# Weight splits moved from GpSimd to VectorE in half tiles, and the weight conversion spread into the second layer

## The chip, the cores and the metric

The kernel runs on one core of one Trainium2 chip. The time is the device time of one execution in microseconds, the lower the better. A core has TensorE (PE), VectorE (DVE), ScalarE (ACT), GpSimd (POOL) and SyncE (SP, which here only issues transfers). Each works through its own instructions in order, and semaphores join them.

## The reference

Three steps follow each other, all with float32 data:

```python
# attention: 4 batches, 8 heads, 576 tokens, head size 64; each query sees the 64 keys up to its own
attn = softmax(where(mask, q @ k.T / 8, -1e9)) @ v          # -> x: 2304 tokens x 512
# experts: a token goes to one of 8; 288 places each, given out in the order of the logits
logits = x @ w_gate                                          # 2304 x 8
assigned = greedy(sorted(logits))
out[assigned == e] = maximum(x[assigned == e] @ w1[e], 0) @ w2[e]      # 512 -> 1024 -> 512
# gated layer
g, val = x @ moe2_w_gate, x @ moe2_w_val                     # 512 -> 1536
return (g * sigmoid(g) * val) @ moe2_w_out                   # 1536 -> 512
```

The three `moe2` weights come as float64 bits and are turned into float32 on the chip.

## The kernel before

The order of all instructions on each engine is the order in which the Python code writes them. There are four stages.

**Attention** (up to about 125 us) makes x, transposed, in `big`, and the logits. The change doesn't touch it.

**Routing** (`routing`, some 125 to 164 us) finds each token's place in six rounds (`step`). A round is a chain of small VectorE steps: `M`, `m`, `below`, `Us`, `u`, `G`; then 18 small TensorE products into `cnt`, then `sat` on VectorE, then two more small products, whose results give VectorE `lt` and ScalarE `cg`, from which GpSimd makes the next `U` (`narrow`). `beside(it)` stands behind each round and holds work that fills gaps: rows of x are transposed and stored to DRAM (`store_rows`), and weights are split. `assign` follows the last round (`oh`, then `ranks`, `places`, `indices`), then a gather of rows by GpSimd, and a branch that is normally not taken.

**Experts** (`experts`, 173 to 401 us): for each of 8 experts `e` and 8 blocks `f` of 128 hidden units, `first(e, f)` makes 12 products of 288 columns into `psw`; ScalarE and VectorE make from it the two parts `hh` and `hl` (`split_psum`). `second` of the `f` before makes 12 products into the four `psa`. At even `f` a piece of the next expert's rows is transposed on TensorE and becomes `xt`.

**Gated layer** (`gated`, 401 to 848 us): three groups `g` of 768 tokens, 12 `f`, two blocks `b` of 384 tokens each. `block` makes 12 products into a `psg` (pg), ScalarE's sigmoid and a VectorE step `sg` read it, then 12 products into the other `psg` (pv), which a second VectorE step reads; ScalarE and VectorE make the two parts of `p`. There are two `psg` banks, so each has to be read before the second product behind it starts. `second` of the `f` before adds 18 products of 512 columns into six `pso`.

Two kinds of work on the weights run beside these stages.

*The split* (`Stream`): every weight matrix is used as two float32r parts, `whi` (a rounded copy by ScalarE) and `wlo` (what is left, a subtraction). A tile of 128x1024 is loaded into one of four `wraw` buffers and split in two halves of 128x512; `whi` and `wlo` have nine buffers each. For the experts' weights the second half's subtraction runs on GpSimd, the first on VectorE; for the gated layer's both run on VectorE. `need(key)` splits up to five tiles ahead of the one asked for. In routing, `beside` splits one tile per round from the second round on, both halves on GpSimd. There are 64 tiles of the experts' weights and 18 of the gated layer's, which are loaded and split anew for each group.

*The conversion* (`convert`, `convert_move`): 36 half pieces of the gated layer's weights; each is loaded as bits (`raw64`), takes four VectorE steps on 128x512 (lines 936 to 942) and a square on ScalarE, and is stored to DRAM, from where the stream loads it. Six steps stand right behind the branch, two or three after each `f` in experts 0 to 6, and `convert_rest` does what is left ahead of expert 7 and closes its buffers.

Of the kernel before, what the change touches and what calls it, by code (L numbers as in the profile page):

```python
# [21 lines left out]
class Stream:  # L22
    """Weights: loaded in float32, split on chip into two float32r parts whose sum is exact."""

    def __init__(self, ctx, tc):
        self.nc = tc.nc
        self.raw = ctx.enter_context(tc.tile_pool(name="wraw", bufs=4))
        self.todo, self.raws, self.parts = [], [], {}
        self.nload = self.nsplit = 0

    def open(self, ctx, tc):
        self.hi = ctx.enter_context(tc.tile_pool(name="whi", bufs=9))
        self.lo = ctx.enter_context(tc.tile_pool(name="wlo", bufs=9))
# [4 lines left out]
    def load(self, upto):  # L38
        while self.nload < min(upto, len(self.todo)):
# [6 lines left out]
    def split(self, upto, engine=None):  # L46
        upto = min(upto, len(self.todo))
        self.load(upto + 4)
        while self.nsplit < upto:
            key, _ = self.todo[self.nsplit]  # L50
            t = self.raws[self.nsplit]
            h = self.hi.tile(list(t.shape), F32R, name="whi")
            lo = self.lo.tile(list(t.shape), F32R, name="wlo")
            for s in range(2):
                if len(t.shape) == 3 and t.shape[1] % 2 == 0:
                    m = t.shape[1] // 2
                    sl = (slice(None), slice(s * m, s * m + m))
# [3 lines left out]
            self.parts[key] = (h, lo)  # L61
            self.nsplit += 1


class Kernel:
# [29 lines left out]

    def attention(self, ctx):
# [16 lines left out]
        # additive masks over [query, (block before, own block)], and without a block before  # L113
# [10 lines left out]
        for i in (1, 5):  # L124
            n = 3
# [16 lines left out]
        # A unit is a window of 64 queries of one pair of heads, hp and hp + HP. A group is four units.  # L142
# [6 lines left out]
        def load_qk(b, name, j):  # L149
            """On the partitions of a quadrant 32 tokens, and 32 of d."""  # L150
# [1037 lines left out]
```

## Time and profile before

| | us |
|---|---|
| runs shown (3) | median 856.53, 856.20 to 856.91 |
| span of the profiled execution, first to last instruction | 854.2 |
| TensorE busy | 796.9 (93%) |
| VectorE busy | 542.7 (64%) |
| ScalarE busy | 383.4 (45%) |
| GpSimd busy | 225.3 (26%) |

The span is the time base of every start in the rows below; the time of a run is some 2.3 us longer than it. A row of a timeline has the start, the length, the engine, the line of the kernel, the operation, the tile written and the tiles read, and the count of instructions that are merged in it; in brackets stands how long the engine was idle just before, and what ended that. TensorE's matmuls overlap, so their lengths add up to more than the distance of their starts.

### The profile page before, as it was taken

How to read it: one execution, taken by the hardware profiler on the slowest of the kernel's cores; microseconds unless marked ns; L12 is line 12 of the kernel's file. 1: busy time of each engine (PE TensorE's matmuls, PEld its weight loads, DVE VectorE, ACT ScalarE, POOL GpSimd, SP SyncE). 2: the span in 40 equal slices, each digit the busy share in tenths (PEclk: the TensorE clock that was granted, in tenths of full speed). 3: DMA queues.
4: the chain of work that ended last, by engine and by line, in shares of the span. 5: the costliest groups of instructions: out<-in, count | busy, mean ns of one | idle time of the engine just before them, and what ended most of it. 6: DMA issues, size and time to landing. Idle time of an engine off the chain costs nothing.

```text
span 854.2 us, 14581 instructions
## 1 busy us (share of the span) xinstructions
PE 796.9 (93%) x5411; PEld 738.6 (86%) x5411; DVE 542.7 (64%) x1014; ACT 383.4 (45%) x980; POOL 225.3 (26%) x263
## 2 busy tenths in 40 slices
PE   5879895499999999999999999999999999999996
PEld 4668774299999999999999999999999999999996
DVE  5868888789999999976443444554344454433422
ACT  4777875356555665666322323433222343221311
POOL 6765745544455444440000000020000002000002
PEclk9999997599999999999999999999999999999998
DMA  9999935679999998855311222241122224101001
GB/s 141 137 142 144 195 113 177 186 243 312 290 318 307 302 315 287 285 187 174 99 29 46 74 74 74 75 149 35 41 74 74 75 74 148 43 32 50 1 1 74
DMA packets 137931, 119.50 MB, mean 140 GB/s; under 512 B 88896, under 2 KB 105280, under 8 KB 137856
## 3 DMA queue, kind: packets, MB, share of 16 engines
q1 hardware_dynamic: 134976, 109.09, 47.2%
q0 software_dynamic: 2880, 9.44, 3.6%
q8 instruction: 44, 0.72, 0.4%
q14 instruction: 31, 0.25, 0.1%
HBM read 99.63 MB, written 18.87 MB: 139 GB/s over the span
## 4 chain that ended last, share of the span: by engine, by line
issue 36%; PE 24%; DVE 16%; POOL 2%; ACT 1%; DMA 0%; POOLq 0%; DVEq 0%; ACTq 0%
PE psg L983 13%; DVE wlo L60 6%; PE pso L983 5%; PE psa L983 3%; PE psw L983 3%; DVE t L940 2%; DVE hl L973 2%; DVE t L938 2%; POOL out_dram L1123 2%; DVE t L936 2%; DVE t L942 1%; DVE xt L976 1%; ACT whi L58 0%; PE psw L1015 0%; DMA w<-t 0%
## 5 line engine op out<-in xcount | busy, mean ns | idle before, releaser
L983 PE MATMUL psg<-y,whi 128*128 128x384 f32 x1152 | 223.1, 336 | 0.0
L983 PEld LDWEIGHTS psg<-y,whi 128*128 128x128 f32 x1152 | 201.6, 188 | 0.0
L1123 POOL DMA_INDIRECT out_dram<-orow,idx x18 | 17.3, 963 | 443.5 <-ACT orow L1121 271.6
L983 PE MATMUL pso<-whi,p 128*128 128x512 f32 x432 | 133.3, 390 | 0.0
L60 DVE TENSOR_TENSOR wlo<-wraw,whi 128x512 fp32r<-128x512 f32 x167 | 129.6, 820 | 4.5 <-ACT whi L58 4.1
L58 ACT ACTIVATE whi<-wraw 128x512 fp32r<-128x512 f32 x236 | 130.4, 620 | 0.1
L60 POOL TENSOR_TENSOR wlo<-wraw,whi 128x512 fp32r<-128x512 f32 x69 | 100.0, 1459 | 103.4 <-ACT whi L58 40.2
L1100 DVE TENSOR_TENSOR sg<-sg,psg 128x384 f32<-128x384 f32 x72 | 39.9, 554 | 131.7 <-ACT sg L1099 131.7
L983 PE MATMUL psg<-y,wlo 128*128 128x384 f32 x576 | 123.4, 336 | 0.0
L1105 ACT ACTIVATE p<-sg 128x384 fp32r<-128x384 f32 x72 | 37.8, 525 | 152.7 <-DVE sg L1103 150.5
L983 PEld LDWEIGHTS psg<-y,wlo 128*128 128x128 f32 x576 | 102.5, 188 | 2.8 <-DVE sg L1100 0.2
L1099 ACT ACTIVATE sg<-psg 128x384 f32<-128x384 f32 x72 | 35.4, 491 | 147.0 <-PE psg L983 147.0
L983 PEld LDWEIGHTS pso<-whi,p 128*128 128x128 f32 x432 | 80.6, 188 | 14.5
L983 PE MATMUL pso<-wlo,p 128*128 128x512 f32 x216 | 84.2, 390 | 0.0
L983 PE MATMUL psa<-hl,whi 128*128 128x288 f32 x256 | 78.4, 306 | 5.2 <-DVE hl L973 4.8
L1103 DVE TENSOR_TENSOR sg<-sg,psg 128x384 f32<-128x384 f32 x72 | 39.9, 554 | 66.5 <-PE psg L983 66.2
L983 PE MATMUL psw<-xt,whi 128*128 128x288 f32 x512 | 78.4, 295 | 0.0
L983 PE MATMUL psa<-hh,whi 128*128 128x288 f32 x256 | 75.4, 295 | 0.0
L983 PE MATMUL psa<-hh,wlo 128*128 128x288 f32 x256 | 75.4, 295 | 0.0
L983 PEld LDWEIGHTS psw<-xt,whi 128*128 128x128 f32 x512 | 71.3, 188 | 0.0
L1106 DVE TENSOR_TENSOR p<-sg,p 128x384 fp32r<-128x384 f32 x72 | 40.2, 559 | 42.6 <-ACT p L1105 42.0
L245 ACT ACTIVATE pp<-ps_s,nm 128x128 f32<-128x128 f32 x144 | 51.0, 369 | 26.8 <-DVE nm L238 24.6
(179 smaller groups left out, 1157.9 us busy)
## 6 DMA issues: line engine op xcount, KB each, us to landing
wraw<-in_moe_w_dram SPq DMA_DIRECT2D x64, 512.0 KB
wraw<-w SPq DMA_DIRECT2D x54, 512.0 KB
w<-t SPq DMA_DIRECT2D x36, 256.0 KB
raw<-in_moe_w_gate_dram SPq DMA_DIRECT2D x12, 512.0 KB
raw<-in_moe_w_val_dram SPq DMA_DIRECT2D x12, 512.0 KB
raw<-in_moe_w_out_dram SPq DMA_DIRECT2D x12, 512.0 KB
vw<-in_v_dram SPq DMA_DIRECT2D x32, 144.0 KB
xrows<-row SPq DMA_DIRECT2D x18, 256.0 KB
```

The source lines that it names most:

```text
L58: self.nc.scalar.activation(h[sl], t[sl], AF.Copy)
L60: eng.tensor_tensor(lo[sl], t[sl], h[sl].bitcast(F32), op=OP.subtract)
L245: nc.scalar.activation(PP[g][:, u, :], ps[:, u, :], AF.Exp, bias=nm[:, u:u + 1], scale=scale, accum_out=SM[g][:, u:u + 1])
L936: nc.vector.tensor_scalar(t, hi, 0x07FFFFFF, 3, op0=OP.bitwise_and, op1=OP.logical_shift_left)
L938: nc.vector.scalar_tensor_tensor(t, hi, -0x40000000, t, op0=OP.bitwise_and, op1=OP.bitwise_or)
L983: self.nc.tensor.matmul(acc, x, y, start=start and i == 0, stop=stop and i == len(seq) - 1)
L1099: nc.scalar.activation(sg, pg, AF.Sigmoid)
L1100: nc.vector.tensor_tensor(sg, sg, pg, op=OP.mult)
L1103: nc.vector.tensor_tensor(sg, sg, pv, op=OP.mult)
L1105: nc.scalar.activation(p[0][:, sl], sg, AF.Copy)
L1106: nc.vector.tensor_tensor(p[1][:, sl], sg, p[0][:, sl].bitcast(F32), op=OP.subtract)
L1123: d = nc.gpsimd.indirect_dma_start(out=self.out, out_offset=bass.IndirectOffsetOnAxis(ap=self.idx[:, 6 * g + t:6 * g + t + 1], axis=0), in ...
```

## The change

- `Stream.split` is taken apart: `half` splits the next half tile, always with ScalarE and VectorE; GpSimd takes no part. `split` calls `half` until enough is done.
- In routing, each of the six rounds has one `half`, written between the products into `cnt` and `sat`. `beside` splits nothing any more, and behind the branch `split(6)` stands where six conversion steps stood.
- `need` runs four tiles ahead in place of five, and `whi` and `wlo` have seven buffers in place of nine. The conversion's buffers stay to the end of the kernel; the rows' buffers (`xg`) are closed ahead of expert 7.
- The conversion has one step after each `f` of all eight experts, and two where `f` is 3 or 7. The rest, four steps each, follows the blocks of the gated layer until it is done. `limit` keeps the stream from loading a piece that is not stored yet.
- The comments and doc lines are gone, which shifts line numbers by some lines.

```diff
     def open(self, ctx, tc):
-        self.hi = ctx.enter_context(tc.tile_pool(name="whi", bufs=9))
-        self.lo = ctx.enter_context(tc.tile_pool(name="wlo", bufs=9))
+        self.hi = ctx.enter_context(tc.tile_pool(name="whi", bufs=7))
+        self.lo = ctx.enter_context(tc.tile_pool(name="wlo", bufs=7))
...
-    def split(self, upto, engine=None):
-        upto = min(upto, len(self.todo))
-        self.load(upto + 4)
-        while self.nsplit < upto:
...
-                self.nc.scalar.activation(h[sl], t[sl], AF.Copy)
-                eng = engine or (self.nc.gpsimd if s and key[0] in ("w1", "w2") else self.nc.vector)
-                eng.tensor_tensor(lo[sl], t[sl], h[sl].bitcast(F32), op=OP.subtract)
+    def half(self):
+        if self.nsplit == len(self.todo):
+            return
+        self.load(self.nsplit + 5)
+        key, _ = self.todo[self.nsplit]
+        t = self.raws[self.nsplit]
+        if key not in self.parts:
+            self.parts[key] = [p.tile(list(t.shape), F32R, name=n) for p, n in ((self.hi, "whi"), (self.lo, "wlo"))]
+        h, lo = self.parts[key]
+        m = t.shape[1] // 2
+        sl = (slice(None), slice(self.nhalf * m, self.nhalf * m + m))
+        self.nc.scalar.activation(h[sl], t[sl], AF.Copy)
+        self.nc.vector.tensor_tensor(lo[sl], t[sl], h[sl].bitcast(F32), op=OP.subtract)
+        self.nhalf = 1 - self.nhalf
+        self.nsplit += not self.nhalf
+
+    def split(self, upto):
+        while self.nsplit < min(upto, len(self.todo)):
+            self.half()
...
             def beside(i):
-                self.st.split(i, self.nc.gpsimd)
                 self.store_rows(3)
                 self.convert_move()
...
                 mm(cnt, G[:, c, :], bl[:, c, :], start=c == 0, stop=c == NT - 1)
+            if it < first:
+                self.st.half()
             nc.vector.tensor_scalar(self.sat[0:32], cnt[:, 0:NE], cnt[:, NE:NE + 1], 0.5 - CAP,
...
+        if self.halves:
+            st.limit = lambda: 8 * NE + self.stored // 2 if self.stored < len(self.halves) else len(st.todo)
...
-        self.st.split(self.order[key] + 5)
+        self.st.split(self.order[key] + 4)
...
         self.convert_move()
-        self.convert(6)
+        self.st.split(6)
...
             if e == NE - 1:
-                self.convert_rest()
+                self.xg_ctx.close()
...
-                if e < NE - 1:
-                    self.convert(n)
-                elif f in (1, 4):
+                self.convert(2 if f % 4 == 3 else 1)
+                if e == NE - 1 and f in (1, 4):
                     self.ready(f // 4)
...
+                self.convert_move()
                 block(g, f, p, 0)
+                self.convert()
                 if f == 11 and g < 2:
                     self.ready(2 * g + 3)
+                self.convert_move()
                 block(g, f, p, 1)
+                self.convert()
```

GpSimd in routing, before: the steps that make the `U` of the third and the fourth round, and the two halves of the first tile between them (`wraw_1485` is the tile, `cg` what the round found).

```order
L673 TENSOR_TENSOR U_2124<-U_2047,cg_2116 128x88
L673 TENSOR_TENSOR U_2124<-U_2047,cg_2116 128x56
L673 TENSOR_TENSOR U_2124<-U_2124,cg_2116 128x88
L673 TENSOR_TENSOR U_2124<-U_2124,cg_2116 128x56
L60 TENSOR_TENSOR wlo_2132<-wraw_1485,whi_2131 128x512 x2
L673 TENSOR_TENSOR U_2209<-U_2124,cg_2201 128x88
```

The same place on GpSimd, after.

```order
L679 TENSOR_TENSOR U_2132<-U_2053,cg_2124 128x88
L679 TENSOR_TENSOR U_2132<-U_2053,cg_2124 128x56
L679 TENSOR_TENSOR U_2132<-U_2132,cg_2124 128x88
L679 TENSOR_TENSOR U_2132<-U_2132,cg_2124 128x56
L679 TENSOR_TENSOR U_2215<-U_2132,cg_2207 128x88
```

Nothing is left on GpSimd between the `U` of one round and that of the next.

VectorE in routing, before: the end of the second round's chain (`below1` marks the experts that are not wanted, `G` the thresholds met).

```order
L608 SCALAR_TENSOR_TENSOR Us_2078<-below1_393,U_2047 128x88
L608 SCALAR_TENSOR_TENSOR Us_2078<-below1_393,U_2047 128x56
L611 TENSOR_REDUCE u_2079<-Us_2078 128x11
L611 TENSOR_REDUCE u_2079<-Us_2078 128x7
L615 TENSOR_TENSOR G_2076<-u_2079,kk_227 128x352
L615 TENSOR_TENSOR G_2076<-u_2079,kk_227 128x224
L652 TENSOR_SCALAR sat_390<-cnt_2090 32x8
```

The same place on VectorE, after.

```order
L612 SCALAR_TENSOR_TENSOR Us_2084<-below1_393,U_2053 128x88
L612 SCALAR_TENSOR_TENSOR Us_2084<-below1_393,U_2053 128x56
L615 TENSOR_REDUCE u_2085<-Us_2084 128x11
L615 TENSOR_REDUCE u_2085<-Us_2084 128x7
L619 TENSOR_TENSOR G_2082<-u_2085,kk_227 128x352
L619 TENSOR_TENSOR G_2082<-u_2085,kk_227 128x224
L60 TENSOR_TENSOR wlo_2035<-wraw_1485,whi_2034 128x512
L658 TENSOR_SCALAR sat_390<-cnt_2096 32x8
```

One half of the first tile now stands between `G` and `sat`.

VectorE in the gated layer's first group, before: the second block of `f` = 1 and the start of `f` = 2.

```order
L1100 TENSOR_TENSOR sg_9071<-sg_9071,psg_9058 128x384
L1103 TENSOR_TENSOR sg_9071<-sg_9071,psg_9074 128x384
L1106 TENSOR_TENSOR p1_9025<-sg_9071,p0_9024 128x384
L60 TENSOR_TENSOR wlo_9093<-wraw_8833,whi_9092 128x512 x2
L60 TENSOR_TENSOR wlo_9127<-wraw_8887,whi_9126 128x512 x2
L60 TENSOR_TENSOR wlo_9135<-wraw_8944,whi_9134 128x512 x2
L1100 TENSOR_TENSOR sg_9153<-sg_9153,psg_9140 128x384
```

The same place on VectorE, after (`t64_8957` is the half piece that is converted, `raw64_8837` its bits, `sq64_8958` its square).

```order
L1098 TENSOR_TENSOR sg_8938<-sg_8938,psg_8925 128x384
L1101 TENSOR_TENSOR sg_8938<-sg_8938,psg_8941 128x384
L1104 TENSOR_TENSOR p1_8879<-sg_8938,p0_8878 128x384
L936 TENSOR_SCALAR t64_8957<-raw64_8837 128x512
L938 SCALAR_TENSOR_TENSOR t64_8957<-raw64_8837,t64_8957 128x512
L940 SCALAR_TENSOR_TENSOR t64_8957<-raw64_8837,t64_8957 128x512
L942 SCALAR_TENSOR_TENSOR t64_8957<-sq64_8958,t64_8957 128x512
L60 TENSOR_TENSOR wlo_8967<-wraw_8664,whi_8966 128x512 x2
L60 TENSOR_TENSOR wlo_9004<-wraw_8719,whi_9003 128x512 x2
L60 TENSOR_TENSOR wlo_9012<-wraw_8781,whi_9011 128x512 x2
L1098 TENSOR_TENSOR sg_9030<-sg_9030,psg_9017 128x384
```

Four conversion steps now stand behind the block's `p`, ahead of the six halves and of the next block's `sg`; the same four stand behind each of 16 blocks.

## Rows read from the trace of the kernel before

**Rows 1.** Busy times: stretch, length, PE, PEld, DVE, ACT, POOL busy (instructions), clock, DMA share, GB/s.

```profile
201.51:375.16 173.65, 168.60 (x1233) 161.41 (x1232) 169.66 (x238) 105.74 (x218) 82.42 (x58) 1.00 0.91 294
...
380.00:400.00 20.00, 19.92 (x150) 19.68 (x149) 14.98 (x20) 11.53 (x24) 3.83 (x4) 1.00 0.50 158
...
400.61:545.60 144.99, 144.99 (x776) 136.96 (x775) 66.51 (x114) 48.08 (x94) 0.00 (x0) 1.00 0.21 66
```

**Rows 2.** Timeline of VectorE in the second expert.

```profile
200.19 1.43 DVE L60 TENSOR_TENSOR wlo<-wraw,whi 128x512 fp32r<-128x512 f32 x1
...
204.38 0.68 DVE L60 TENSOR_TENSOR wlo<-wraw,whi 128x512 fp32r<-128x512 f32 x1
```

**Rows 3.** Timeline of GpSimd in the same stretch.

```profile
199.78 1.30 POOL L60 TENSOR_TENSOR wlo<-wraw,whi 128x512 fp32r<-128x512 f32 x1 [4.11 <-ACT whi L58]
201.44 1.33 POOL L60 TENSOR_TENSOR wlo<-wraw,whi 128x512 fp32r<-128x512 f32 x1 [0.37 <-POOL wlo L60]
```

**Rows 4.** Timeline of VectorE in the gated layer, `f` = 1 and 2.

```profile
415.93 0.56 DVE L1100 TENSOR_TENSOR sg<-sg,psg 128x384 f32<-128x384 f32 x1 [0.96 <-ACT sg L1099]
417.43 0.56 DVE L1103 TENSOR_TENSOR sg<-sg,psg 128x384 f32<-128x384 f32 x1 [0.94 <-PE psg L983]
418.58 0.56 DVE L1106 TENSOR_TENSOR p<-sg,p 128x384 fp32r<-128x384 f32 x1 [0.59 <-ACT p L1105]
419.10 3.70 DVE L60 TENSOR_TENSOR wlo<-wraw,whi 128x512 fp32r<-128x512 f32 x6
424.18 0.55 DVE L1100 TENSOR_TENSOR sg<-sg,psg 128x384 f32<-128x384 f32 x1 [1.39 <-ACT sg L1099]
```

**Rows 5.** Timeline of VectorE in routing.

```profile
126.88 0.22 DVE L652 TENSOR_SCALAR sat<-cnt 32x8 bf16<-32x8 f32 x1 [0.47 <-PE cnt L651]
...
128.45 0.68 DVE L604 TENSOR_TENSOR below<-M,m 128x88 bf16<-128x88 f32 x2
129.04 0.41 DVE L608 SCALAR_TENSOR_TENSOR Us<-below,U 128x88 f32<-128x88 bf16 x2
...
130.89 0.22 DVE L652 TENSOR_SCALAR sat<-cnt 32x8 bf16<-32x8 f32 x1 [0.43 <-PE cnt L651]
...
132.99 2.52 DVE L608 SCALAR_TENSOR_TENSOR Us<-below,U 128x88 f32<-128x88 bf16 x2
...
155.10 0.22 DVE L652 TENSOR_SCALAR sat<-cnt 32x8 bf16<-32x8 f32 x1 [0.44 <-PE cnt L651]
...
156.42 1.45 DVE L683 TENSOR_TENSOR oh<-M,m 128x88 bf16<-128x88 f32 x2
```

**Rows 6.** Timeline of ScalarE in routing.

```profile
125.15 1.57 ACT L467 ACTIVATE row<-rowps 128x512 f32<-128x512 f32 x3 [1.45 <-PE rowps L465]
...
131.49 1.14 ACT L58 ACTIVATE whi<-wraw 128x512 fp32r<-128x512 f32 x2
```

**Rows 7.** Timeline of VectorE behind the branch: first steps of two half pieces.

```profile
168.06 0.43 DVE L936 TENSOR_SCALAR t<-raw 128x512 int32<-128x512 int32 x1 [3.88 <-DVEq L710]
...
170.67 0.42 DVE L936 TENSOR_SCALAR t<-raw 128x512 int32<-128x512 int32 x1
```

**Rows 8.** Groups of instructions by line and shape: busy us, mean ns of one | idle before.

```profile
L973 DVE SCALAR_TENSOR_TENSOR hl<-psw,hh 128x288 fp32r<-128x288 f32 x64 | 28.8, 451 | 8.2 <-ACT hh L972 7.9
...
L976 DVE TENSOR_TENSOR xt<-psw,xt 128x512 fp32r<-128x512 f32 x12 | 8.1, 681 | 0.5 <-issue 0.5
```

**Rows 9.** TensorE in the experts: a piece of the chain, and its timeline around a transpose.

```profile
389.46 1.59 PE psw L983 x12
...
181.60 0.29 PE L983 MATMUL psa<-hl,whi 128*128 128x288 f32 x1
...
182.22 0.79 PE L983 MATMUL psw<-xt,wlo 128*128 128x288 f32 x4
```

**Rows 10.** Timeline of TensorE at `f` = 2: the second block's first products.

```profile
425.48 0.86 PE L983 MATMUL psg<-y,wlo 128*128 128x384 f32 x4
```

More of the change, by code (lines that the diff above doesn't have):

```diff
@@ L28, in __init__ @@
         self.todo, self.raws, self.parts = [], [], {}
-        self.nload = self.nsplit = 0
+        self.nload = self.nsplit = self.nhalf = 0
+        self.limit = lambda: len(self.todo)
     def open(self, ctx, tc):
-        self.hi = ctx.enter_context(tc.tile_pool(name="whi", bufs=9))
-        self.lo = ctx.enter_context(tc.tile_pool(name="wlo", bufs=9))
+        self.hi = ctx.enter_context(tc.tile_pool(name="whi", bufs=7))
+        self.lo = ctx.enter_context(tc.tile_pool(name="wlo", bufs=7))
     def add(self, key, src):
@@ L38, in load @@
     def load(self, upto):
-        while self.nload < min(upto, len(self.todo)):
+        while self.nload < min(upto, self.limit()):
             key, src = self.todo[self.nload]
@@ L44, in load @@
             self.nload += 1
-    def split(self, upto, engine=None):
-        upto = min(upto, len(self.todo))
-        self.load(upto + 4)
-        while self.nsplit < upto:
[L50 to L57, printed above, removed]
-                self.nc.scalar.activation(h[sl], t[sl], AF.Copy)
-                eng = engine or (self.nc.gpsimd if s and key[0] in ("w1", "w2") else self.nc.vector)
-                eng.tensor_tensor(lo[sl], t[sl], h[sl].bitcast(F32), op=OP.subtract)
-            self.parts[key] = (h, lo)
-            self.nsplit += 1
+    def half(self):
[16 more added lines that the diff above has]
+            self.half()
 class Kernel:
@@ L499, in build @@
         self.st.open(self.ctx, tc)
-        self.xg_p, self.xg = self.conv.enter_context(tc.tile_pool(name="xg", bufs=4, side="right")), {}
+        self.xg_ctx = ExitStack()
+        self.xg_p, self.xg = self.xg_ctx.enter_context(tc.tile_pool(name="xg", bufs=4, side="right")), {}
         with ExitStack() as ctx:
@@ L883, in weights_setup @@
             self.pieces["wo", j] = wo[:, 2 * j:2 * j + 2, :]
-        self.halves, self.cv, self.ct, self.conv = [], {}, {}, ExitStack()
+        self.halves, self.cv, self.ct = [], {}, {}
         self.nconv = self.part = self.stored = self.loaded = 0
@@ L888, in weights_setup @@
         dram = self.pool("wdram", 1, bass.MemoryType.DRAM)
-        self.cp = self.conv.enter_context(self.tc.tile_pool(name="conv", bufs=2, side="right"))
+        self.cp = ctx.enter_context(self.tc.tile_pool(name="conv", bufs=2, side="right"))
         for key in ((n, j) for j in range(6) for n in ("wg", "wv", "wo")):
@@ L897, in weights_setup @@
             self.pieces[key] = t
-    def convert_rest(self):
-        while self.stored < len(self.halves):
-            self.convert_move()
-            self.convert()
-        self.conv.close()
     def convert_move(self, queue=None):
@@ L1054, in experts @@
             for f in range(8):
-                if e < NE - 1:
-                    self.convert_move()
+                self.convert_move()
                 h = first(e, f)
@@ L1060, in experts @@
                 late = (e, f, h)
-                n = 3
                 if todo and f % 2 == 0:
                     transposed(*todo.pop(0))
-                    n = 2
-                if e < NE - 1:
-                    self.convert(n)
-                elif f in (1, 4):
+                self.convert(2 if f % 4 == 3 else 1)
+                if e == NE - 1 and f in (1, 4):
                     self.ready(f // 4)
@@ L1133, in gated @@
                 p = [p_p.tile([128, 2 * n], F32R, name=f"p{i}") for i in range(2)]
+                self.convert_move()
                 block(g, f, p, 0)
+                self.convert()
                 if f == 11 and g < 2:
                     self.ready(2 * g + 3)
+                self.convert_move()
                 block(g, f, p, 1)
+                self.convert()
                 if f == 6 and g < 2:
```

## The prediction

> **What bounds the kernel now.** I read the page's slices first, then the busy times of each engine by stage, then the timelines of VectorE, GpSimd and TensorE inside the stages. The whole-span shares mix three stages with different limits, so they decide nothing here. In the gated layer TensorE is never idle and VectorE works 66.5 of 145 us, with GpSimd at zero; in the six experts between 201.51 and 375.16 VectorE is busy 169.66 of 173.65 us, while TensorE is not full (168.60, and its busy time hides short gaps because matmuls overlap) [rows 1]. In routing a chain of small VectorE steps sets the pace.
>
> Then I looked at what makes VectorE so busy. A `wlo` half (128x512 subtraction) that starts at 200.19 takes 1.43 us; GpSimd's own `wlo` half runs from 199.78 to 201.08, and VectorE's ends 0.54 after it [rows 2, 3]. At 204.38, with GpSimd's next half over at 202.77, one takes 0.68 [rows 2, 3], and six in a row in the gated layer take 3.70, 0.617 each [rows 4]. So a VectorE step with two SBUF inputs that meets a GpSimd subtraction waits for its end: one half on GpSimd costs VectorE up to 1.3 us, more than doing it itself (0.617). The same in routing: the two `Us` steps take 0.41 in the first round and 2.52 in the second, where the splits stand beside them [rows 5].
>
> **The change part by part.** *Routing.* Removed: the two GpSimd halves of each round. The distance of two `sat` steps is 4.01 in the first round, where nothing disturbs, and (155.10 - 130.89) / 4 = 6.05 in the four others [rows 5]. Added: ahead of each `sat` one `wlo` half on VectorE, which sat idle 0.43 there [rows 5]: 0.617 - 0.43 = 0.19 late, taken as 0.25 with the hand-over. In the first round the half waits for its `whi` behind three row copies that end at 126.72: 0.57 more for `whi` [rows 6] and 0.617 put `sat` at some 127.95 instead of 126.88. So the sixth `sat` comes at 127.95 + 5 x 4.26 = 149.25 instead of 155.10: -5.8. The `oh` steps (1.45) lose GpSimd's last halves and fall to the 0.68 of the same shape [rows 5]: -0.8. Sum **-6.6**; bounds -8.0 (all halves but the first hidden) and -4.8 (each costs its full length). The row stores queue on SP behind the loads, as before: the load of tile 4 now waits for the half of the second round, and rows 3 to 8 behind it; a row copy needs its slot of six back only a round later, so I cost this at nothing; if it fails, ScalarE's `cg` is late by a store, some 1 us.
>
> *Behind the branch.* Six conversion steps (four take 170.67 - 168.06 = 2.61 [rows 7], six 3.9) make room for six halves (6 x 0.617 = 3.7): zero, at worst one half, +0.6.
>
> *Experts.* 59 GpSimd halves become VectorE halves of 0.617, and conversion falls from 20 or so steps per expert to 10. VectorE's work per expert: 16 halves 9.9, eight `hl` at 0.451 3.6, three `xt` at 0.681 2.0 [rows 8], ten conversion steps at 2.61 / 4 [rows 7] 6.5; sum 22, against 169.66 / 6 = 28.3 now [rows 1]. TensorE's own need: 16 groups of 1.59 [rows 9] make 25.4, and each piece of rows that is transposed adds 0.49 (the next product starts at 182.22 instead of 181.60 + 1.59 / 12) [rows 9]. Six experts hold 19 pieces: 6 x 25.44 + 9.3 = 161.9, against the 173.65 from the first `hh` of expert 1 to that of expert 7 [rows 1]: -11.7 if no wait is left. VectorE at 22 of 27 is 81% full; in the last expert it was at 75%, and TensorE ran without a gap (19.92 of 20) [rows 1]. If the loss of 1.95 per expert at 98% fell in a straight line to 0 at 75%, 0.5 would remain: -8.7. I take **-10.7**, nearer to the undisturbed row, since no `f` gets more than two halves, an `hl`, and an `xt` with one step or two steps alone: 1.23 + 0.45 + 1.33 = 3.0 us, under TensorE's 3.18. The first expert stays out. SP has fewer transfers here; the 7 split slots in place of 9 with one tile less ahead still leave a slot free three steps before it is filled.
>
> *Gated layer, first group.* 80 of 144 conversion steps are done by then; the other 64 come as four after each of 16 blocks, `f` = 0 to 7, 2.61 us each [rows 7] on the engine that also frees the two `psg` banks. Follow `f` = 1 and 2 of before [rows 4]: after block 0 VectorE had 0.96 idle before the `sg` step at 415.93, so four steps put that at 417.58, and the next (417.43) at 418.14, 0.7 late; the `p` steps follow 0.7 late. After block 1 stand four steps and then the six halves; idle there was 1.39. The `sg` step at 424.18 comes 0.7 + 2.61 - 1.39 = 1.9 late and ends at 426.6; TensorE wants its bank at 425.48 [rows 10]: 1.2 late. In odd `f` no halves stand in front, and the output product hides the steps. So 1.2 at `f` = 2, 4, 6 and 8, and about 1.2 in `f` = 0 and 1, which have no output product between them: **+6**. Bounds: 0, if the steps fit into other gaps, and +9. Loads keep ahead: three tiles or more are loaded before their split, so the way of a piece through DRAM is hidden; behind the waiting loads on SP stand only others of the kind.
>
> [...]
>
> **Sum.** -6.6 - 10.7 + 6 = -11.3, against the profile's own span of 854.2: 842.9. The median of the runs shown is 856.53, 2.3 more than the span; that lies outside the stages and stays. Forecast: **845.2 us**.
>
> **The rivals.** *The conversion is hidden in the gated layer.* VectorE is idle over half of that stage [rows 1], which speaks for it; that it does its steps in order, ahead of a bank's release, speaks against it. 845.2 - 6 = 839.2.
>
> *The experts keep part of their waits.* VectorE at 81% in order, `hl` behind two halves and a conversion step; with the gain at half, -5.4, the time is 850.5. The last expert's full TensorE speaks against it [rows 1].
>
> *The conversion doesn't fit in the gated layer* (slower). VectorE's own work per pair of `f`, 4 x (2.61 + 3 x 0.56) + 3.7 = 20.9, and four waits of 0.59 for ScalarE's `p` [rows 4] make 23.2 of the 24.2 that TensorE needs (144.99 / 6 [rows 1]). If a further wait, for the loads of `raw64` or for `sq` on ScalarE, fills the rest, each block pays. At the full 2.61 for 16 blocks it is 41.8: 856.5 - 17.3 + 41.8 = 881. From 17.3 / 16 = 1.1 us per block on, the change is slower than before. The loads standing two halves (12 us) ahead speak against it.
>
> *Moving work between GpSimd and VectorE gives nothing.* If the long steps came from the transfers (0.91 of the DMA engines there, 0.21 in the gated layer [rows 1]), halves on VectorE would stay long, routing and experts would gain nothing, and only the cost would be left: 856.5 + 6 = 862.5. The 0.68 at 204.38, amid the same transfers, speaks against it [rows 2]. [...]
>
> **How the numbers follow.** Forecast 0.63; hidden 0.13; half the gain 0.13; doesn't fit 0.08; nothing gained 0.03. The bounds of the terms move the forecast from about 839 (-8.0 - 11.7 + 3) to 851 (-4.8 - 8.7 + 8). The range 838.5 to 852 takes in these, the hidden case and most of the half gain, and leaves out the two slower cases and a tail. A measurement of this kernel tells about 0.2% (1.7 us) from no change; above 858.2 lie the two last rivals, 0.10 with a tail; between 854.8 and 858.2 about 0.04; below it 0.86.
>
> **What would show it.** Right: `sat` steps some 4.3 apart; `wlo` halves of VectorE at 0.6 to 0.7 everywhere; 27 us per expert and TensorE waiting for `hl` almost never; in the gated layer waits of 1 us for the `psg` bank at even `f` up to 8, none from then on. Wrong: VectorE steps still over 1 us in the experts, row copies that wait for stores, or a ScalarE that stands at `sq` or `whi` for a load in the first group, which would push every block.

## The result and the profile after

The changed kernel takes **847.06 us** (median of four executions, 842.39 to 849.46), the kernel before 856.37 (856.04 to 856.91): a ratio of 0.988, 95% interval 0.986 to 0.991. The forecast was 845.2, range 838.5 to 852. The profiled execution is the shortest of the four, 842.39 us with a span of 840.6. A second profile of the same kernel, from the first experiment, has a span of 845.8, and both are used below.

The page's busy times and its costliest group of VectorE, after the change (the group's columns: busy us, mean ns of one, idle before):

```profile
PE 788.9 (94%) x5411; PEld 734.4 (87%) x5411; DVE 526.4 (63%) x1083; ACT 383.9 (46%) x980; POOL 123.3 (15%) x194
...
L60 DVE TENSOR_TENSOR wlo<-wraw,whi 128x512 fp32r<-128x512 f32 x236 | 149.6, 687 | 8.8 <-DVEq L716 3.8
```

All 236 halves are on VectorE now and last 0.687 us in the mean. The 1.43 of [rows 2] is gone.

Read by stage, with the same marks in each profile (the marks are the last `U` step of the attention, the sixth `sat`, `idx`, the first `hh` and the first `psg` product):

| stretch, us | before | after | after, second profile | forecast of the difference |
|---|---|---|---|---|
| start to the last `U` step | 121.8 | 120.7 | 121.8 | 0 |
| to the sixth `sat` | 33.3 | 27.5 | 28.7 | -5.8 |
| to `idx` | 8.7 | 7.6 | 7.6 | -0.8 |
| to the first `hh` | 11.2 | 11.8 | 14.2 | 0 |
| to the first `psg` product | 225.5 | 213.4 | 213.9 | -10.7 |
| to the end | 453.7 | 459.6 | 459.6 | +6 |
| span | 854.2 | 840.6 | 845.8 | -11.3 |

**Routing.** The timeline of VectorE after the change, around the second to the fourth `sat`, against [rows 5] (start, length, engine; in brackets the idle time before and what ended it):

```profile
130.21 0.69 DVE L60 TENSOR_TENSOR wlo<-wraw,whi 128x512 fp32r<-128x512 f32 x1
130.81 0.21 DVE L658 TENSOR_SCALAR sat<-cnt 32x8 bf16<-32x8 f32 x1
...
132.90 0.41 DVE L612 SCALAR_TENSOR_TENSOR Us<-below,U 128x88 f32<-128x88 bf16 x2
...
134.44 0.69 DVE L60 TENSOR_TENSOR wlo<-wraw,whi 128x512 fp32r<-128x512 f32 x1
135.05 0.21 DVE L658 TENSOR_SCALAR sat<-cnt 32x8 bf16<-32x8 f32 x1
...
139.47 0.69 DVE L60 TENSOR_TENSOR wlo<-wraw,whi 128x512 fp32r<-128x512 f32 x1 [0.75 <-ACT whi L59]
140.08 0.21 DVE L658 TENSOR_SCALAR sat<-cnt 32x8 bf16<-32x8 f32 x1
```

`Us` takes 0.41 where [rows 5] had 2.52, and two `sat` steps are 4.24 apart, as forecast. The next two are 5.03 apart: here the half waits 0.75 for `whi`. That wait is new, and the runs below follow it.

**Experts.** Busy times from the first `hh` of expert 1 to that of expert 7, against the first of [rows 1]:

```profile
193.66:356.99 163.33, 163.33 (x1240) 161.58 (x1239) 123.63 (x225) 97.96 (x205) 9.54 (x11) 1.00 0.77 246
```

163.33 us instead of 173.65; VectorE is busy 123.63 of them, 20.6 per expert, and TensorE waits for nothing.

**Gated layer.** TensorE at `f` = 2, in its timeline after the change, where [rows 10] had no wait, and the next products:

```profile
406.16 1.55 PE L985 MATMUL psg<-y,whi 128*128 128x384 f32 x8
408.71 0.97 PE L985 MATMUL psg<-y,wlo 128*128 128x384 f32 x4 [1.00 <-DVE sg L1098]
409.52 1.54 PE L985 MATMUL psg<-y,whi 128*128 128x384 f32 x8
410.90 0.86 PE L985 MATMUL psg<-y,wlo 128*128 128x384 f32 x4
411.59 1.55 PE L985 MATMUL psg<-y,whi 128*128 128x384 f32 x8
```

and VectorE just ahead of it, against [rows 4]:

```profile
403.89 0.69 DVE L942 SCALAR_TENSOR_TENSOR t<-sq,t 128x512 f32<-128x512 f32 x1
404.50 3.69 DVE L60 TENSOR_TENSOR wlo<-wraw,whi 128x512 fp32r<-128x512 f32 x6
408.11 0.55 DVE L1098 TENSOR_TENSOR sg<-sg,psg 128x384 f32<-128x384 f32 x1
```

The last conversion step, the six halves and the `sg` step that frees the bank follow each other without idle time, so TensorE waits. It does so six times: at `f` = 2, 4, 6 and 8, and twice in `f` = 0 and 1. Such a wait costs more than its idle time, since matmuls otherwise overlap: from 406.16 to 408.71 are 2.55 us, where the same groups stand 1.38 apart without a wait (409.52 to 410.90), although the first of them lasts 1.54, and the next group starts 0.81 later instead of 0.69. So 1.00 of idle time costs 1.29.

### The profile page after: what moved, and what is told of

The parts are those of the page before. It is cut to its first block, busy times and chain, and to the rows that moved or that the text cites. A ratio compares the mean times of both kernels' runs of the same rounds, so it can differ in the third digit from the quotient of the medians.

```text
span 840.6 us, 14411 instructions
## 1 busy us (share of the span) xinstructions
PE 788.9 (94%) x5411; PEld 734.4 (87%) x5411; DVE 526.4 (63%) x1083; ACT 383.9 (46%) x980; POOL 123.3 (15%) x194
## 4 chain that ended last, share of the span: by engine, by line
PE 38%; issue 34%; DVE 7%; POOL 2%; DMA 1%; ACT 1%; POOLq 0%; DVEq 0%
PE psw L985 12%; PE psa L985 12%; PE psg L985 9%; PE pso L985 4%; DVE wlo L60 2%; POOL out_dram L1121 1%; PE psw L1017 1%; DVE t L938 1%; DVE t L940 1%; DVE sg L1101 1%; DMA xg<-xrows,idx 1%; ACT p L1103 1%; DVE t L942 1%; DVE t L936 1%; DVE sg L1098 1%
## 5 line engine op out<-in xcount | busy, mean ns | idle before, releaser
L60 DVE TENSOR_TENSOR wlo<-wraw,whi 128x512 fp32r<-128x512 f32 x236 | 149.6, 687 | 8.8 <-DVEq L716 3.8
L985 PE MATMUL psa<-hl,whi 128*128 128x288 f32 x256 | 75.5, 295 | 0.0
L249 ACT ACTIVATE pp<-ps_s,nm 128x128 f32<-128x128 f32 x144 | 50.9, 365 | 26.2 <-DVE nm L242 24.2
L974 ACT ACTIVATE hh<-psw 128x288 fp32r<-128x288 f32 x64 | 26.3, 411 | 61.8 <-PE psw L985 60.5
```

The source lines that it names most:

```text
L60: self.nc.vector.tensor_tensor(lo[sl], t[sl], h[sl].bitcast(F32), op=OP.subtract)
L249: nc.scalar.activation(PP[g][:, u, :], ps[:, u, :], AF.Exp, bias=nm[:, u:u + 1], scale=scale, accum_out=SM[g][:, u:u + 1])
L974: nc.scalar.activation(h, x, AF.Relu)
L985: self.nc.tensor.matmul(acc, x, y, start=start and i == 0, stop=stop and i == len(seq) - 1)
```

## Experiments

Each kernel is an edit of the changed kernel and was timed beside the kernel before on the same chip (856.25, 856.25, 855.92 and 855.65 us in the four sets of runs).

### The changed kernel again

No edit.

> The changed kernel once more, without an edit: its first four executions lay between 842.4 and 849.5 us, those of the kernel before within 0.9. Theory A (the start and the attention, whose clock varies): the spread stays, median 845 to 848, and in the new trace the stages from routing on repeat to 0.5 us (sat steps 4.0 to 5.0 apart, 163.3 us from the first hh of expert 1 to that of expert 7, 459.5 us from the first psg product to the end); what differs lies before the first sat step. Theory B (the fit in experts or gated layer is tight, and transfers that come a little later cost waits): the stretch from expert 1 to 7 or the gated layer is 3 to 6 us longer than in the first trace. Theory C (the stretch behind the branch, where the granted clock was 0.61): the time between the last routing step and the first expert product varies by several us.

Measured: 846.50 us (843.14 to 850.00, six executions). No one theory holds alone. B falls: experts and gated layer repeat to 0.5 us. The attention ends 1.1 us later than in the first profile (A), the stretch behind the branch takes 2.4 longer (C), and routing, which I had taken as fixed, is 1.1 longer to the sixth `sat`. The distances of the `sat` steps are 4.22, 5.03, 4.19, 4.07 and 5.03, against 4.03, 4.24, 5.03, 4.06 and 4.06 in the first profile. Counted by the distances of the `sat` steps, ScalarE in the first round of the second profile (4.22) and the second (5.03):

```profile
129.02 1.10 ACT L471 ACTIVATE row<-rowps 128x512 f32<-128x512 f32 x2 [0.40 <-PE rowps L469]
130.38 0.60 ACT L471 ACTIVATE row<-rowps 128x512 f32<-128x512 f32 x1 [0.26 <-PE rowps L469]
130.88 0.62 ACT L59 ACTIVATE whi<-wraw 128x512 fp32r<-128x512 f32 x1
133.71 0.60 ACT L471 ACTIVATE row<-rowps 128x512 f32<-128x512 f32 x1 [0.86 <-PE rowps L469]
134.56 0.60 ACT L471 ACTIVATE row<-rowps 128x512 f32<-128x512 f32 x1 [0.26 <-PE rowps L469]
135.41 0.60 ACT L471 ACTIVATE row<-rowps 128x512 f32<-128x512 f32 x1 [0.26 <-PE rowps L469]
135.91 0.62 ACT L59 ACTIVATE whi<-wraw 128x512 fp32r<-128x512 f32 x1
```

The busy times of TensorE in the rounds of the second profile (length, PE busy, granted clock, DMA share, GB/s):

```profile
127.92:132.14 4.22, 2.81 (x33) 0.65 0.19 73
132.14:137.17 5.03, 3.62 (x33) 0.61 0.78 247
137.17:141.36 4.19, 2.31 (x33) 1.00 0.56 210
141.36:145.43 4.07, 2.61 (x33) 0.69 0.67 184
145.43:150.46 5.03, 3.63 (x33) 0.50 0.72 273
```

The long rounds are those with 3.6 us of TensorE work, granted 0.50 to 0.61 (0.50 is the lowest clock in any of these tables); so is the one of the first profile (3.62 us, 0.62). The clock varied in the kernel before too, 0.96 in its second round and 0.50 in its third, with no effect on their 6 us. The two, and the long round of the first profile:

```profile
130.89:137.00 6.11, 2.32 (x33) 0.96 0.17 51
137.00:143.00 6.00, 3.63 (x33) 0.50 0.66 213
```

```profile
135.05:140.08 5.03, 3.62 (x33) 0.62 0.61 227
```

What is new is the way from the clock to `sat`: twelve transposes (2.82 us in the long round of the first profile, 1.53 to 2.04 in its other rounds), three row copies, `whi` behind them on ScalarE, `wlo`, and behind it `sat`. This is the theory of the later runs.

### The experts: each part undone alone, and both

Second halves of the experts' tiles back on GpSimd, from the seventh tile on:

```diff
-        self.nc.vector.tensor_tensor(lo[sl], t[sl], h[sl].bitcast(F32), op=OP.subtract)
+        eng = self.nc.gpsimd if self.nhalf and self.nsplit >= 6 and key[0] in ("w1", "w2") else self.nc.vector
+        eng.tensor_tensor(lo[sl], t[sl], h[sl].bitcast(F32), op=OP.subtract)
```

> The changed kernel, with the second half of every first-layer weight tile from the seventh on back on GpSimd; routing and conversion stay as changed. My theory (a GpSimd subtraction holds up VectorE steps with two SBUF inputs, so 8 halves per expert cost VectorE 8 x (1.3 - 0.617) = 5.5 us more than doing them itself): VectorE's work rises from 20.5 to 26 of 26.9 us per expert, wlo halves of 1.2 to 1.4 us on VectorE are back, and an expert takes 27.5 to 28.5: 850 to 857 us. Rival (fewer conversion steps alone freed the experts, and where the splits run does not matter): 26.9 per expert as before, 847 us, although single steps are long.

Measured: 846.64 us (843.68 to 848.56). My theory fell, the rival holds. Its stretch from expert 1 to 7, and VectorE's halves there:

```profile
198.29:361.61 163.32, 163.32 (x1240) 161.57 (x1239) 135.95 (x177) 97.93 (x204) 90.79 (x58) 1.00 0.76 245
```

```profile
L61 DVE TENSOR_TENSOR wlo<-wraw,whi 128x512 fp32r<-128x512 f32 x49 | 56.9, 1162 | 3.6 <-ACT whi L59 2.1
```

The long halves are back: 1.16 us for one on VectorE, where the changed kernel has 0.69 in this stretch. It does not cost a microsecond of the whole, because VectorE, at 22.7 us per expert, still has room. I had expected 5.5 us more per expert on VectorE; it is 2.1 ((135.95 - 123.63) / 6).

Conversion at the old pace, 20 or 21 steps per expert, none left for the gated layer:

```diff
             todo = pieces(e + 1) if e + 1 < NE else []
+            npieces = len(todo)
...
-                self.convert(2 if f % 4 == 3 else 1)
+                self.convert(2 if f % 2 == 0 and f < 2 * npieces else 3)
```

> The changed kernel, with 20 or 21 conversion steps per expert as in the kernel before, so that none is left for the gated layer; all splits stay on VectorE. My theory (VectorE's sum decides in the experts): 20.5 + 10.5 x 0.65 = 27.3 us of VectorE work against 26.9 of TensorE, so 27.5 to 28.5 per expert, 4 to 11 us lost over seven experts, against 6 us gained in the gated layer, whose waits at even f vanish: 845 to 852. Rival (the contention with GpSimd was the whole trouble, the number of steps mattered little): experts stay near 27.0 and the whole is 847 - 6 = 841.

Measured: **839.46 us** (837.32 to 842.53), 7 us under the changed kernel on the same chip. The rival holds again. Its stretch from expert 1 to 7:

```profile
196.81:359.25 162.44, 162.44 (x1234) 160.69 (x1233) 157.81 (x289) 106.70 (x221) 10.11 (x11) 1.00 0.93 318
```

VectorE is busy 97% of the time, and TensorE waits for nothing: a queue that is nearly full costs nothing here, as long as its sum stays under TensorE's. From the first `psg` product to the end it takes 453.4 us, as before the change.

Both edits together, the two diffs above:

> The changed kernel with both parts undone in the experts only: second halves of the weight tiles on GpSimd, and 20 or 21 conversion steps per expert, so that none is left for the gated layer; seven split slots and the routing stay as changed. With the two runs that undo one part each (163.3 and 162.4 us from the first hh of expert 1 to that of expert 7, no wait of TensorE) this fills the fourth field of the table. My theory (either part alone takes VectorE below its limit, both undone put it back over it): VectorE busy 97% or more of about 173 us in that stretch, TensorE waiting for hl again, gated layer 453.5 us: whole 849 to 852. Rival (the smaller number of slots, or another step that was made behind the splits, made the gain): the stretch stays at 163 us and the whole is 839 to 841.

Measured: 852.51 us (850.80 to 855.13, seven executions), half a microsecond above the range of my theory, and its mechanism is there. Busy times from expert 1 to 7, and TensorE's waits there (total, times, longest):

```profile
196.90:370.50 173.60, 168.10 (x1228) 160.74 (x1227) 171.62 (x240) 106.64 (x220) 80.04 (x58) 1.00 0.90 299
```

```profile
PE psa L986 <- DVE hl L976: 5.0, 12, 0.7
```

The stretch is the 173.65 of [rows 1] again, so neither the slots nor another step made the gain. The four fields, VectorE's work per expert (a sixth of the row) and the time from the first `hh` to the first `psg` product:

| | 10 steps per expert | 20 or 21 steps |
|---|---|---|
| all splits on VectorE | 20.6 us; 213.4 and 213.9 | 26.3 us; 213.4 |
| second halves on GpSimd | 22.7 us; 214.3 | 28.6 us; 226.3 |

TensorE needs 27.2 per expert here (163.33 / 6). Only the field above that pays. Either part of the change brings the whole gain of the experts; the second brings nothing more. Eight halves per expert on GpSimd add 2.1 to 2.3 us to VectorE's work, 0.26 to 0.29 for each, although VectorE no longer makes them.

### Gated layer: the same steps at other places

```diff
                 block(g, f, p, 0)
-                self.convert()
+                self.convert(4 if f % 2 else 5)
...
                 block(g, f, p, 1)
-                self.convert()
+                self.convert(0 if f % 2 else 7)
```

> The changed kernel, with the conversion steps of the gated layer as 5, 7, 4, 0 after the four blocks of a pair of f instead of 4, 4, 4, 4, so that none stands directly ahead of the six halves. My theory (four steps and six halves in one queue make TensorE wait 1.0 to 1.25 us at f = 2, 4, 6 and 8): these waits vanish or fall below 0.4, the gated layer is 4 to 5 us shorter (455 instead of 459.5 us), whole 842 to 843. Rival 1 (each step costs wherever it stands): the waits move to other blocks, the gated layer stays at 459 to 460, whole 847. Rival 2 (seven steps after one block wait for their loads of raw64): a wait of over 1 us on VectorE at raw64 or t64, whole 848 or more.

Measured: 846.39 us (844.43 to 846.51); the gated layer takes 458.9 us instead of 459.6. TensorE's waits in it:

```profile
PE psg L985 <- DVE sg L1098: 4.8, 3, 2.5
```

Three waits instead of six. Those at `f` = 2, 4, 6 and 8 are gone, as my theory says. But TensorE waits 0.89 and 2.48 in `f` = 0 and 1, where no output product hides the seven steps, and 1.42 in `f` = 7, where a `y` split (two steps, 1.82 us) stands in the same queue behind seven others. The expected time did not come: the steps cost where nothing covers them, and I had moved some to such places. Rival 1 is right on the time and in that the waits move; that a step costs wherever it stands is wrong, since none of those that an output product covers does.

### Routing: where the halves are made

As in the kernel before, two halves per round on GpSimd, ten in all:

```diff
             def beside(i):
+                self.st.engine = self.nc.gpsimd
+                self.st.split(i)
+                self.st.engine = None
...
-            if it < first:
-                self.st.half()
```

> The changed kernel with the routing splits as in the kernel before: both halves of a tile on GpSimd in each of five rounds, ten in all; behind the branch only two halves are left instead of six; experts and gated layer as changed. With one GpSimd half per round (run r_gps) the sixth sat came 23.4 us after the first and the whole took 845.4 us. My theory (two halves fill GpSimd's gap between the U steps, so that one of them always meets the chain on VectorE): rounds of 5.8 to 6.2 us, the sixth sat 27 to 28.5 us after the first; up to 1 us given back behind the branch; whole 849 to 852. Rival 1 (the rounds were slow in the kernel before for another reason, such as the loads or the nine slots): rounds of 4 to 5 us, whole 844 to 847. Rival 2 (what the rounds lose, the stretch behind the branch gains, with four halves fewer there): whole 845 to 847 in spite of rounds of 6.

Measured: 849.44 us (848.51 to 855.41, seven executions), my theory. In whole times that is 2.9 us above the changed kernel (846.50), on a chip on which the kernel before is 0.6 shorter. The sixth `sat` comes 27.7 us after the first, rounds from the second on are 5.9 to 6.1, and `Us` takes 2.53 again:

```profile
131.88 2.53 DVE L617 SCALAR_TENSOR_TENSOR Us<-below,U 128x88 f32<-128x88 bf16 x2
```

One half per round on GpSimd, at the place where the changed kernel has it:

```diff
-        self.nc.vector.tensor_tensor(lo[sl], t[sl], h[sl].bitcast(F32), op=OP.subtract)
+        eng = self.nc.gpsimd if self.nsplit < 3 else self.nc.vector
+        eng.tensor_tensor(lo[sl], t[sl], h[sl].bitcast(F32), op=OP.subtract)
```

> The changed kernel, with the six halves of the routing rounds on GpSimd instead of VectorE (one per round; the kernel before had two per round); everything behind the branch as changed. My theory (a VectorE step with two SBUF inputs that meets a GpSimd subtraction waits for its end): single steps of the chain such as Us, M or u last up to 1.3 us again in each round, rounds last 4.8 to 5.5 us at either clock, the sixth sat comes 24 to 27.5 us after the first, whole 848 to 851. Rival (as in the experts, the place of the splits does not matter): the sixth sat after 21 to 24 us as with VectorE, whole 846 to 847.

Measured: 845.44 us (843.98 to 848.74), the rival. Rounds of 5.65, 3.95, 4.51, 5.34 and 3.99. GpSimd's timeline has two halves in the first, none in the second, one in the third, two in the fourth and none in the fifth (the sixth half falls behind the last `sat`): every round with a half pays, 0.6 to 0.9 for each, and those without one are short. VectorE and GpSimd in the first round, where `M` takes 0.55 and `G` 0.83 when no half stands beside them:

```profile
128.62 1.29 DVE L673 SCALAR_TENSOR_TENSOR M<-lt,L 128x88 f32<-128x88 f32 x2
...
131.29 1.72 DVE L620 TENSOR_TENSOR G<-u,kk 128x352 bf16<-128x352 bf16 x2
```

```profile
128.23 1.28 POOL L61 TENSOR_TENSOR wlo<-wraw,whi 128x512 fp32r<-128x512 f32 x1 [7.70 <-ACT whi L59]
...
131.06 1.26 POOL L61 TENSOR_TENSOR wlo<-wraw,whi 128x512 fp32r<-128x512 f32 x1 [0.37 <-ACT whi L59]
```

The sixth `sat` comes 23.4 us after the first, as in the profiles of the changed routing (21.4 to 24.2). So much of the routing's gain came from one half per round instead of two, and not from the engine.

No halves in the rounds, six more behind the branch:

```diff
-            if it < first:
-                self.st.half()
```

> The changed kernel with no split in the routing rounds: the six halves are made behind the branch, with the six that are there already. My theory: without a half ahead of sat nothing ties a round to the row copies, so rounds last 4.0 to 4.2 us at either clock and the sixth sat comes 20 to 21 us after the first; behind the branch twelve halves take 7.4 us on VectorE instead of 3.7, of which the wait for the gather hides some: the first expert product comes 11.5 to 14 us after idx instead of 10 to 11.5; whole 845 to 848. Rival (half clock makes a round long by its own matmuls): rounds of 5 stay and the whole is 849 to 851.

Measured: 847.95 us (846.74 to 849.94), as expected in the sum, not in the stretch behind the branch. Rounds of 3.95 to 4.04, at either clock (TensorE in the first and the last round):

```profile
127.77:131.72 3.95, 2.31 (x33) 1.00 0.84 314
...
143.64:147.68 4.04, 3.62 (x33) 0.50 0.38 139
```

This shows that a round at the lower clock is not long by its own matmuls. What routing gained is given back behind the branch: the first expert product comes 14.9 us after `idx`, where I expected 14 at most, and the first `hh` after 18.1 (11.8 and 14.2 in the two profiles of the changed kernel), since the tiles' loads could not run ahead of the splits (ScalarE):

```profile
165.49 1.15 ACT L59 ACTIVATE whi<-wraw 128x512 fp32r<-128x512 f32 x2 [5.61 <-DMA wraw<-in_moe_w_dram]
```

### Routing without the tie to the row copies, and the best of both

`whi` ahead of the row copies. `half()` gets an argument with which it issues ScalarE's copy alone; the later call leaves the copy out:

```diff
+        if self.ahead != (self.nsplit, self.nhalf):
+            self.nc.scalar.activation(h[sl], t[sl], AF.Copy)
+            self.ahead = self.nsplit, self.nhalf
+        if high:
+            return
...
+            self.st.half(high=True)
             self.store_rows(3)
             def beside(i):
+                if i < 5:
+                    self.st.half(high=True)
                 self.store_rows(3)
```

> The changed kernel, with ScalarE's copy whi of a routing round's half issued ahead of the three row copies instead of behind them; VectorE's wlo half stays ahead of sat. My theory (a round lasts 5.03 us instead of 4.03 to 4.24 where TensorE's granted clock is 0.50 to 0.65 throughout, because sat stands behind wlo, wlo behind whi, whi behind three row copies, and these behind twelve transposes that take 2.8 us there instead of 2.0): no wlo half of routing waits for whi any more, every round lasts 4.0 to 4.3 us at either clock, the sixth sat comes 20.1 to 21.5 us after the first (21.4 to 24.2 in the five traces so far), the median falls by 1.5 to 3 to 843.5 to 845, and the executions lie closer together. Rival 1 (at half clock the matmuls for cnt, low and tot are the longer chain): rounds of 5.0 stay, 846.5. Rival 2 (the rows come later, so the gather waits): rounds short, but the first expert product comes no sooner, 846.5.

Measured: 848.83 us (846.09 to 854.17): none of the gain that I expected, and 2.3 us above the changed kernel, where the executions of the two overlap. Neither rival names what happened. No half waits for `whi` any more, but two rounds last 6.17 and 5.99. The new first step also issues the load of the fifth tile, ahead of the first three row stores on SP, and that load waits for a slot until the second `sat`. SP, and the row copy that needs the store:

```profile
132.65 0.37 SPq L43 DMA_DIRECT2D wraw<-in_moe_w_dram  x1
133.13 5.03 SPq L479 DMA_DIRECT2D xrows<-row  x6
```

```profile
137.56 0.60 ACT L477 ACTIVATE row<-rowps 128x512 f32<-128x512 f32 x1 [3.80 <-DMA xrows<-row]
```

Behind that copy stands `cg`, behind `cg` GpSimd's `U`, and behind `U` VectorE's `Us`, which waits 2.46 us:

```profile
140.73 0.48 DVE L621 SCALAR_TENSOR_TENSOR Us<-below,U 128x88 f32<-128x88 bf16 x2 [2.46 <-POOL U L688]
```

It is the accident that the prediction priced at 1 us; it did not happen in the changed kernel, and here it cost 2 us a time.

The same edit with the conversion at the old pace:

> Both changes that the runs so far point to: ScalarE's whi of the routing rounds ahead of the row copies, and 20 or 21 conversion steps per expert with all splits on VectorE, none in the gated layer. My theory: the gains add: 839.5 of the second alone less 1.5 to 3, 836.5 to 838. Rival (what routing gains is lost behind the branch, where the gather ends last): 839.5.

Measured: 839.82 us (837.02 to 842.64): the time of the early conversion alone. The rival's number, though not for its reason: two rounds lasted 5.7 and 6.0 us here too.

The same edit once more, with the load left where it was:

```diff
-        self.load(self.nsplit + 5)
+        if not high:
+            self.load(self.nsplit + 5)
```

> ScalarE's whi ahead of the row copies as in the run early_whi, but with the weight loads issued where the changed kernel issues them, behind the row stores, since there a row copy waited 3.8 us for a store that stood behind a load. My theory: rounds of 4.0 to 4.25 us at either clock, sixth sat 20.1 to 21.3 us after the first, no wait of VectorE for U or whi over 0.3 us, median 843 to 845 with the executions closer together. Rival (the copies, now behind whi, hold up cg or the stores in another way): a round of 5 us or more is left, median 846 to 848.

Measured: **841.89 us** (840.89 to 844.09), a little better than expected, 0.984 of the kernel before (0.982 to 0.986). Rounds of 4.03 to 4.11 us, with TensorE at either clock (its first and third round):

```profile
126.58:130.61 4.03, 2.31 (x33) 1.00 0.46 171
...
134.64:138.75 4.11, 3.62 (x33) 0.50 0.81 303
```

The sixth `sat` comes 20.3 us after the first, and the five executions lie within 3.2 us, the ten of the changed kernel within 7.6. That the rounds make this difference is not shown: the four executions with shifted steps, whose routing is the changed kernel's, lie within 2.1.

And with the conversion at the old pace:

> The run before and 20 or 21 conversion steps per expert with all splits on VectorE, none in the gated layer. My theory: 839.5 less what the rounds gain, 1.5 to 3: 836.5 to 838. Rival (the rounds gain nothing in the median, since the stretch behind the branch gives it back): 839.5.

Measured: **835.54 us** (833.79 to 837.22), 0.975 of the kernel before (0.973 to 0.978) and some 11 us under the changed kernel. It keeps the splits on VectorE, leaves the conversion in the experts, and takes `whi` out from behind the row copies. First and last `psg` product, of this kernel, of the changed one and of the kernel before (min/median/max ns, first and last start):

```profile
L995 PE MATMUL psg<-y,whi x1152: 332/336/338, 381.0 to 819.0; 128*128 128x384 f32 x192
```

```profile
L985 PE MATMUL psg<-y,whi x1152: 332/336/338, 381.7 to 826.0; 128*128 128x384 f32 x192
```

```profile
L983 PE MATMUL psg<-y,whi x1152: 332/336/338, 401.1 to 839.1; 128*128 128x384 f32 x192
```

438.0 us here, 444.3 in the changed kernel, and 438.0 in the kernel before.

## Why the prediction was right, and where it was not

**What bounds the kernel.** Right for the experts, and shown by the fourth field of the table: VectorE's sum over TensorE's. Right in routing as far as GpSimd's halves go (the run with two halves per round). The price of a half on GpSimd, up to 1.3 us of VectorE's time where doing it itself takes 0.617, is that of single rows; over the experts it is 0.26 to 0.29 more than doing it itself.

**Routing, -6.6.** Measured from the last `U` step of the attention to `idx`: -6.8 and -5.7 in the two profiles of the changed kernel, and in four other profiles with the same routing -5.1 (shifted steps), -5.1 (early conversion), -4.1 (second halves on GpSimd in the experts) and -4.1 (both). The first `sat` came 1.0 to 1.1 us late as worked out, the `Us` steps lost what was forecast, and the `oh` steps lost 1.07 (from 1.45 to 0.38) instead of 0.8. The step that failed is the equal rounds of 4.26: they are 4.03 to 4.24, or 5.02 to 5.04. I had written that the half waits for `whi` behind the row copies, in the first round alone; it does so again, for 0.74 to 0.92 us, in each long round of all six profiles, and in no other. In the three of them whose TensorE was read by rounds (both of the changed kernel and that with shifted steps) the long rounds are those with 3.62 or 3.63 us of TensorE work, granted 0.50 to 0.62. One such round costs 0.8 to 1.0, and the six profiles, in the order above, have one, two, three, three, four and four of them. The two with four lie past my bound of -4.8, and the first profile is the luckiest of the six.

**Behind the branch, 0.** Measured +0.6 and +3.0, and 11.3 to 14.2 us from `idx` to the first `hh` in the profiles of kernels that are alike there (15.7 and 15.8 in the two with the early load). In the second profile of the changed kernel (14.2), two pieces of gathered rows are transposed and the third comes 1.61 us later, and the first product's `whi` matmuls take 2.08, where they take 1.21 in the first profile at a granted 1.00. Whether the gather starts it or the clock (0.64 in the mean from 158.10 to 170.30) is left open; no run was made on it.

**Experts, -10.7.** Measured -10.3 over the same stretch, and -12.1 and -11.6 with the first expert, which I had left out. The size is right. VectorE's 22 us per expert were 20.6, mostly since a conversion step took 0.53 (34.2 us more for 64 steps more) instead of 0.65. Two things in the reasoning are wrong. I summed both parts of the change into one term, and never asked what each alone would do: each alone does it all. And the bound by a loss that falls in a straight line with VectorE's share (-8.7) has no ground: at 97% there is none. By the fourfold table halves on GpSimd leave VectorE with more to do, 22.7 us per expert against 20.6. The rival in which nothing is gained (862.5) put the long steps down to the transfers, and it fell: a half on VectorE lasts 0.69 us at a DMA share of 0.93 (conversion at the old pace), and 1.16 at 0.76 with the second halves on GpSimd.

**Gated layer, +6.** Measured +5.9 twice, at the places named and for the reason named: waits of 0.90 to 1.00 at `f` = 2, 4, 6 and 8 and 0.98 together in `f` = 0 and 1. They add up to 4.7 of idle time. By the starts of the groups, as worked out for `f` = 2 above, the six cost 6.3 (1.29, three times 1.17, 0.84 and 0.69), and the distance of the first `psg` product from the last grew by the same 6.3. The early conversion takes the 6 us away, and shifting the steps moves the waits. A half by itself lasts 0.69 us in the rows above, but the next step starts 0.60 later (130.21 to 130.81), and six take 3.69, 0.615 each: for a sum the distance counts.

**The sum.** -11.3 forecast; -13.6 and -8.4 in the two profiles, -9.3 in the medians. The number held, in part by luck, since two errors offset each other. In medians the runs part the change so: routing and what stands behind it -3.4 (852.51 with both parts undone in the experts, against 855.92; 95% interval -4.8 to -1.5), experts -13.0 (852.51 to 839.46), and gated layer +7.0 (839.46 to 846.50); the -13.0 compares runs of two sets on two chips, where the kernel before differs by 0.3. So the forecast took too much for routing and too little for the experts, where it had left out the first one. The bounds of its terms were also not all counted: it took +3 and +8 for the gated layer, where it had given 0 and +9; with these the forecast moves from 837 to 852, not from 839 to 851. Of the two parts that relieve VectorE in the experts only one was needed: with the splits on VectorE and the conversion at its old pace 839.5, with both parts 846.5. The rival in which the conversion is hidden gave 839.2; that time is reached by leaving the conversion in the experts, not by hiding it.

## What to carry to other kernels

When two parts of a change relieve the same engine, price each alone as well: here VectorE cost TensorE nothing at 97% of the stretch, and 11 us when its sum passed TensorE's, so the second relief only carried its own cost. When work is put ahead of a critical step on one engine, follow all that it waits for back through the other queues, in every round and at the lower clock (0.50 to 0.62 here) too. When an instruction is moved up, look at the loads that its helper issues with it.

## What the runs showed of the hardware

TensorE's granted clock in routing differs from one execution to the next in the same round: between the third and the fourth `sat` it was 0.62 and 1.00 in the two profiles of the changed kernel, and 0.50 in that of the kernel with shifted steps, whose routing is the same. The kernel before hid it (rounds of 6.11 us at 0.96 and of 6.00 at 0.50); the changed one passes it on as 0.8 to 1.0 us per round.

GpSimd's half lasted 1.26 to 1.28 us in routing (one half per round) and 1.70 in the mean in the experts (second halves on GpSimd, 81.0 us for 48), where VectorE's steps stand beside it; that the two hold each other up in both directions fits this, but no run separates it. What GpSimd's halves do to VectorE's steps depends on the step. In the experts, with 20 or 21 conversion steps and with and without GpSimd's halves, the means are 1.04 and 0.69 us for a half, 0.85 to 1.01 and 0.69 for the conversion steps with two inputs, and 0.63 and 0.42 for that with one; `hl` (0.45 both times) and `xt` (0.68 and 0.69), which read one input from PSUM, stay as they are.
